# Lightning attention and an ELU layer on one core: attention in 64-token blocks on 64x64 tiles of TensorE

## The chip, the cores and the metric

The kernel runs on one core of a Trainium2 chip. The metric is the device time of one execution in microseconds (us); less is better. A core has TensorE (PE in the profile, its weight loads PEld), VectorE (DVE), ScalarE (ACT), GpSimd (POOL) and SyncE (SP, which here only starts transfers). Matmuls write PSUM, which has eight banks of 128 partitions x 512 float32.

## The reference

Four batches, eight heads, 768 tokens, 64 dimensions a head. Attention with a decay `lam` per head runs over blocks of 64 tokens and carries a 64x64 state per head; its output, 3072 tokens of 512, goes through two matrix products with an ELU between them.

```python
Dmask = np.where(rel >= 0, lam[:, None, None] ** rel[None, :, :], 0.0)
lam_pow = lam[:, None, None] ** (pos[None, :, None] + 1)
for b in range(nb):                       # nb = 768 // 64
    intra = np.einsum('bhic,bhjc->bhij', qb, kb) * Dmask[None]
    intra = np.einsum('bhij,bhjd->bhid', intra, vb)
    inter = np.einsum('bhid,bhde->bhie', qb * lam_pow[None], kv_state)
    out[:, :, sl] = intra + inter
    kb_dec = kb * rev_pow[None]           # lam ** (63 - pos)
    kv_state = lam_block * kv_state + np.einsum('bhsd,bhse->bhde', kb_dec, vb)
x = attn_out.transpose(0, 2, 1, 3).reshape(3072, 512)
h = x @ w_in                              # 512 x 2048
g = np.where(h > 0.0, h, np.exp(np.minimum(h, 0.0)) - 1.0)
out = g @ w_out                           # 2048 x 512
```

The block length of the decay is free: with the mask and the decays made for it, blocks of 128 tokens give the same result as blocks of 64.

## The kernel before

The tokens are cut into 24 chunks of 128. Chunk `g` is place `g // 4` in the sequence of batch `g % 4`, so chunks 0 to 3 are the first of each batch and have no state to read. The program is one long string of words, `PROGRAM`, written out in the order in which instructions are handed to the engines; every engine takes its own in that order, and waits at each until its operands and its buffer are there. A letter names the step and the number the chunk; what stands after `@` is the PSUM bank.

For one chunk:

- `Lq`, `Lk`, `Lv` load queries, keys and values with a cast to float16, started on POOL's queue (L240), for one chunk or for two at a time. `H` and `C` load one raw on SP and cast it on an engine. `wi`, `wo` load the weights in eight pieces each (L245, L251).
- `T` transposes q and k on PE (L264), and `tq`, `tk` take them out of PSUM (L272, L276). From chunk 8 on, transposing transfers on SP's queue do this (`Dq`, `Dk`, L280).
- `S`: scores, per head a 64x128 by 128 matmul (L287). Two heads lie one above the other in the 128 partitions, so a pair uses the upper and the lower half of the array's rows, and writes two banks. `s`: the decay mask, on DVE (L294).
- `P`: masked scores by values (L304), and the state by q (L310). Both give 64 columns of output a head, and a pair of heads uses the left and the right half of the array's columns. `p`: the result times `qs` into `xt`, on DVE (L328), or a copy on ACT where `tq` has scaled q already (L326).
- `kd`: keys times their decay, on POOL (L332). `U`: the update of the state, keys by values (L366, 64 columns; L354 on the whole array). `M`: the state times its decay, on POOL (L342). `u`: their sum, on DVE (L381).

Then for a group of chunks (`GROUPS`: the first four alone, the others two by two): `A`, the first product (L392), eight matmuls of 256 columns into one bank for a group of two; `x`, exp on ACT (L400); `r`, relu in place on ACT (L403); `m`, the ELU from both, on DVE (L408), into one of 40 `g` buffers. `B`, the second product (L422), four matmuls of 512 columns of one chunk. `o` takes the result out of PSUM (L431), `st` stores it from SP's queue. The last chunk is cut in 384 and 128 columns, the latter being `R` (L445).

`A` alternates between two banks of its own (tag `H`), `B` between `M0` and `M1`, and attention uses `A` to `D`. The loads wait for their buffers on POOL's queue in the order of the string, between `kd` and `M`; the transposing transfers and the stores do so on SP's.

Of the kernel before, what the change touches and what calls it, by code (L numbers as in the profile page):

```python
# [7 lines left out]
FP32 = mybir.dt.float32  # L8
FP16 = mybir.dt.float16
# [5 lines left out]
GROUPS = [(0, 1), (1, 1), (2, 1), (3, 1), (4, 2), (6, 2), (8, 2), (10, 2), (12, 2), (14, 2), (16, 2), (18, 2), (20, 2), (22, 2)]  # L15

LOADS = [(0, 1), (1, 1), (2, 1), (3, 1), (4, 2), (6, 2), (8, 2), (10, 2), (12, 2), (14, 2), (16, 2), (18, 2), (20, 2), (22, 2)]

BUFS = {'qn1': 4, 'kn1': 4, 'vn1': 4, 'qn2': 4, 'kn2': 4, 'vn2': 4, 'qT': 5, 'kT': 5, 'pp': 6, 'kd': 8, 'stt': 8, 'xt1': 4, 'xt2': 2, 'xt4': 2, 'e': 3, 'g': 40, 'osb512': 4}

ON = {'z0.0', 'z2.0', 'z1.0', 'o23', 'z3.0'}
# [67 lines left out]
def kernel(  # L89
# [14 lines left out]
    L = 128  # L104
    NHP = H // 2
# [4 lines left out]
    FB = 4  # L110
# [4 lines left out]
    load_of = {g + i: (g, i) for g, n in LOADS for i in range(n)}  # L115
    load_n = dict(LOADS)
    words = PROGRAM.split()
    scaled = {int(w[2:]) for w in words if w[:2] == "tq"}
# [12 lines left out]
    st = [[const(f"st{b}_{i}", [128, NHP, 128], FP16) for i in range(2)] for b in range(B)]  # L131
# [4 lines left out]
    pos = const("pos", [128, 3])  # L136
    row = const("row", [128, 128])
    ident16 = const("ident16", [128, 128], FP16)
    causT = const("causT", [128, 128])
    dn = const("dn", [128, H])  # L140
    mask = const("mask", [128, H, 128])
    qs = const("qs", [128, NHP, 128])
    ks = const("ks", [128, H])
    upp = const("upp", [128, NHP])
# [8 lines left out]
    R = [slice(0, 64), slice(64, 128)]  # L153
    nat, raw, tr, psT, psS, pp, psO, xg = {}, {}, {}, {}, {}, {}, {}, {}
    kds, stt, psU, psH, es, gts, psM, osb = {}, {}, {}, {}, {}, {}, {}, {}
    done = set()
# [4 lines left out]
    def bank(tag, shape, dtype, name):  # L161
        return ps.tile(shape, dtype, tag=f"ps{tag}", name=name, bufs=2 if tag == "H" else 1)
# [8 lines left out]
    def make_qs(_):  # L171
        for hp in range(NHP):
            nc.scalar.activation(
                qs[:, hp, :], row[:], AF.Exp, scale=loglam_p[:, hp : hp + 1]
            )
# [5 lines left out]
    simple = {  # L181
        "lam": lambda _: nc.sync.dma_start(
            out=lam_b[:], in_=lam.unsqueeze(0).broadcast_to([128, H])
        ),
        "tab": lambda _: nc.scalar.preload_act_table_set("natural_log_exp_and_others"),
# [35 lines left out]
    def of(w, g):  # L221
        g0, i = load_of[g]
        return nat[w, g0][:, i]
# [303 lines left out]
```

## Time and profile before

| | |
|---|---|
| median of 3 runs | 214.75 us (214.7 to 216.03) |
| profiled execution, time | 215.01 us |
| profiled execution, span | 213.2 us |
| granted TensorE clock | 1.0 |
| PE busy | 199.2 us, 2048 matmuls |
| DVE busy | 129.6 us, 223 instructions |
| ACT busy | 127.9 us, 245 instructions |
| POOL busy | 96.6 us, 115 instructions |
| HBM read, written | 27.27 MB, 6.29 MB |

The span runs from the first to the last instruction of the profiled execution; its time is 1.8 us more. A row of a group has the line of the kernel, the engine, the operation, output and inputs by name with their shapes, and the count; then the busy time in us, the mean duration in ns, and how long the engine was idle just before these instructions, with what ended most of that. A row of the timeline has start and length in us, engine and line, and `xN` where N of a kind were merged. A row by stretches has the busy time of PE, PEld, DVE, ACT and POOL in it (each with its count), then the clock, the DMA share and GB/s. Ends of matmuls are modelled; their starts are recorded.

### The profile page before, as it was taken

The page shows a single profiled execution, that of the slowest core. Times are in us where ns is not written, and L with a number is a line of the kernel's source. Part 1 is how long each engine was busy: PE and PEld are TensorE (multiplying, and loading weights), DVE is VectorE, ACT ScalarE, POOL GpSimd, SP SyncE. Part 2 cuts the span into 40 slices and gives each one's busy share as a digit, 9 for nine tenths or more (in the row PEclk, how much of TensorE's full clock was granted, in tenths as well). Part 3 has the DMA queues.
Part 4 walks back from the last instruction along what each step waited for, and adds up shares of the span by engine and source line. Part 5 has one row for each costly group of instructions (what it writes and reads, how often), then busy time and mean ns, then how long its engine had stood idle before and what let it go on. Part 6 is the DMA issues. An engine that isn't in the chain of part 4 may idle for free.

```text
span 213.2 us, 5052 instructions
## 1 busy us (share of the span) xinstructions
PE 199.2 (93%) x2048; PEld 138.5 (65%) x2048; DVE 129.6 (61%) x223; ACT 127.9 (60%) x245; POOL 96.6 (45%) x115
## 2 busy tenths in 40 slices
PE   0599989999999999999989999999999999999994
PEld 0378767677677766767657677667666776666662
DVE  3877764385877866788538676366558665353321
ACT  4436766568776765585554865665674565556731
POOL 7999965599994995376902691000000000000000
PEclk9999999999999999999999999999999999999999
DMA  5999999999999999969997999146110000021042
GB/s 95 152 181 184 197 194 182 158 145 151 161 120 166 127 169 150 148 101 113 187 148 80 158 187 127 25 130 145 25 52 0 0 16 36 3 103 46 0 152 98
DMA packets 101976, 24.59 MB, mean 115 GB/s; under 512 B 92608, under 2 KB 99008, under 8 KB 101952
## 3 DMA queue, kind: packets, MB, share of 16 engines
q0 software_dynamic: 79760, 13.50, 83.5%
q1 hardware_dynamic: 22192, 10.76, 23.9%
q8 instruction: 16, 0.26, 0.5%
q14 instruction: 8, 0.07, 0.1%
HBM read 27.27 MB, written 6.29 MB: 157 GB/s over the span
## 4 chain that ended last, share of the span: by engine, by line
PE 64%; POOL 17%; DMA 15%; issue 1%; ACT 0%; SPq 0%; POOLq 0%
PE psM L422 29%; PE psH L392 28%; DMA kn<-in_k_dram 5%; DMA vn<-in_v_dram 4%; DMA qT<-qn 4%; POOL wi L245 3%; POOL kn L240 3%; POOL wo L251 3%; POOL kd L332 3%; DMA out_dram<-osb 3%; POOL qn L240 3%; PE psO L304 2%; POOL vn L240 2%; PE psO L310 2%; PE psS L287 2%
## 5 line engine op out<-in xcount | busy, mean ns | idle before, releaser
L408 DVE SCALAR_TENSOR_TENSOR g<-e,psH 128x512 f16<-128x512 f32 x96 | 65.6, 685 | 61.3 <-ACT psH L403 61.0
L392 PE MATMUL psH<-xt,wi 128*128 128x256 f16 (+1 forms) x896 | 97.6, 259 | 0.9 <-DMA wi<-in_moe_w_in_dram 0.8
L400 ACT ACTIVATE e<-psH 128x512 f32<-128x512 f32 x96 | 57.2, 596 | 67.4 <-PE psH L392 67.0
L422 PE MATMUL psM<-wo,g 128*128 128x512 f16 (+1 forms) x384 | 92.7, 377 | 0.2 <-ACT osb L431 0.2
L392 PEld LDWEIGHTS <-wi 128*128 128x128 f16 x896 | 77.5, 99 | 22.8 <-DMA wi<-in_moe_w_in_dram 1.3
L403 ACT ACTIVATE psH<-psH 128x512 f32<-128x512 f32 x96 | 56.9, 594 | 0.0
L422 PEld LDWEIGHTS <-g 128*128 128x128 f16 x384 | 36.4, 98 | 31.4 <-issue 0.4
L294 DVE TENSOR_TENSOR pp<-psS,mask 128x512 f16<-128x512 f32 x48 | 31.4, 682 | 7.6 <-PE psS L287 7.5
L332 POOL TENSOR_TENSOR kd<-kn,ks 128x512 f16<-128x512 f16 x20 | 20.8, 1049 | 13.0 <-DMA kn<-in_k_dram 12.5
L342 POOL TENSOR_TENSOR stt<-st,upp 64x256 f32<-64x256 f16 x32 | 19.6, 612 | 7.4 <-DVE st L381 5.9
L240 POOL DMA_DIRECT2D vn<-in_v_dram x14 | 15.7, 1121 | 9.0 <-PE psO L310 9.0
L431 ACT COPY osb<-psM 128x512 f32<-128x512 f32 x23 | 13.4, 588 | 5.7 <-PE psM L422 4.8
L240 POOL DMA_DIRECT2D kn<-in_k_dram x14 | 15.5, 1107 | 1.6 <-DMA wi<-in_moe_w_in_dram 1.4
L240 POOL DMA_DIRECT2D qn<-in_q_dram x13 | 14.4, 1110 | 0.1
L381 DVE TENSOR_TENSOR st<-stt,psU 64x256 f16<-64x256 f32 x32 | 13.0, 415 | 0.8 <-PE psU L366 0.3
L304 PE MATMUL psO<-pp,vn 128*64 128x128 f16 x192 | 12.5, 229 | 0.3 <-DMA vn<-in_v_dram 0.3
L304 PEld LDWEIGHTS <-vn 128*64 128x64 f16 x192 | 10.0, 114 | 2.6 <-issue 1.6
L328 DVE TENSOR_TENSOR xt<-psO,qs 128x512 f16<-128x512 f32 x16 | 10.7, 683 | 1.1 <-PE psH L392 0.6
L287 PE MATMUL psS<-qT,kT 64*128 64x128 f16 x192 | 8.4, 228 | 2.8 <-DMA qT<-qn 1.1
L310 PE MATMUL psO<-qT,st 128*64 128x128 f16 x160 | 10.3, 219 | 0.0
L287 PEld LDWEIGHTS <-kT 64*128 64x128 f16 x192 | 5.9, 98 | 5.8 <-issue 3.6
L310 PEld LDWEIGHTS <-st 128*64 128x64 f16 x160 | 9.0, 110 | 0.0
(45 smaller groups left out, 65.1 us busy)
## 6 DMA issues: line engine op xcount, KB each, us to landing
out_dram<-osb SPq DMA_DIRECT2D x23, 256.0 KB, 2.9
qn<-in_q_dram POOLq DMA_DIRECT2D x10, 256.0 KB, 8.0
kn<-in_k_dram POOLq DMA_DIRECT2D x10, 256.0 KB, 6.5
vn<-in_v_dram POOLq DMA_DIRECT2D x10, 256.0 KB, 7.0
wi<-in_moe_w_in_dram POOLq DMA_DIRECT2D x8, 256.0 KB, 6.4
wo<-in_moe_w_out_dram POOLq DMA_DIRECT2D x8, 256.0 KB, 7.4
kn<-in_k_dram POOLq DMA_DIRECT2D x4, 128.0 KB, 4.7
vn<-in_v_dram POOLq DMA_DIRECT2D x4, 128.0 KB, 5.5
```

The lines of the kernel that those rows point to most:

```text
L240: nc.gpsimd.dma_start(out=t[:].rearrange("p b h d -> p (b h) d"), in_=source(w, g0, load_n[g0]))
L287: nc.tensor.matmul(psS[g, hh][:, hp, :], lhsT=tr["k", g][r, hp, :], rhs=tr["q", g][r, hp, :], start=True, stop=True,)
L294: nc.vector.tensor_tensor(out=p[:], in0=psS.pop((g, hh))[:], in1=mask[:, hh::2, :], op=ALU.mult)
L304: nc.tensor.matmul(po[r, hp, :], lhsT=of("v", g)[:, 2 * hp + hh, :], rhs=pp[g, hh][:, hp, :], start=True, stop=(cb == 0), skip_group_check ...
L310: nc.tensor.matmul(po[r, hp, :], lhsT=st[b][cb % 2][:, hp, r], rhs=tr["q", g][:, hp, :], start=False, stop=True, skip_group_check=True,)
L332: nc.gpsimd.tensor_tensor(out=kds[g][:], in0=of("k", g), in1=ks[:].unsqueeze(2).broadcast_to([128, H, 64]), op=ALU.mult,)
L342: nc.gpsimd.tensor_tensor(out=t[r], in0=st[b][cb % 2][r, :, r], in1=upp[r].unsqueeze(2).broadcast_to([64, NHP, 64]), op=ALU.mult,)
L392: nc.tensor.matmul(pH[:, f * n * 128 : (f + 1) * n * 128], lhsT=wi16[i][:, kk, w * 128 : (w + 1) * 128], rhs=xg[g0][:, kk, :], start=(kk = ...
L400: nc.scalar.activation(es[g0, j][:], psH[g0, j][:], AF.Exp)
L403: nc.scalar.activation(psH[g0, j][:], psH[g0, j][:], AF.Relu)
L408: nc.vector.scalar_tensor_tensor(out=g[:].rearrange("p f c t -> p (f c t)"), in0=es.pop((g0, j))[:], scalar=-1.0, in1=psH.pop((g0, j))[:], ...
L422: nc.tensor.matmul(psM[g][:, cols], lhsT=gts[g, f], rhs=wo16[i][:, w, cols], start=f == 0, stop=f == NFT - 1, skip_group_check=True,)
```

## The change

Attention goes over to blocks of 64 tokens. Two chunks (two batches at the same place) are handled together, and in each the two halves of 64 tokens:

- A transpose takes the same head of both chunks, so the two batches lie one above the other in the 128 partitions (`transpose`, and `transpose_dma` in two halves). q, k are loaded chunk by chunk into interleaved tiles, v by two.
- Scores, masked scores by values, state by q and updates are matmuls of 64 rows, 64 columns of weights and 64 columns of data. Four in a row use the four quarters of the array. A chunk's mask is one operation of 512 in place of two.
- The state exists for each block of 64: `u` and `M` come twice per pair of chunks, each over all 128 partitions.
- In the first chunks no state is read: the second half of the tokens sees the first through a score block of its own (`mask1` for the whole 128 keys, `z` for the first half).
- `Q` is the state by q for one assignment of halves, ahead of `P`; `F`, a copy of one column on DVE, stands between them.
- All groups are of two chunks. 31 of the 96 relus go to DVE, 7 of the `o`, 6 of the 12 `kd`. All PSUM tiles share eight banks that the string names one by one.
- `W`: 36 products with zeros on PE in the opening.
- The whole order is new.

```diff
-GROUPS = [(0, 1), (1, 1), (2, 1), (3, 1), (4, 2), (6, 2), (8, 2), (10, 2), (12, 2), (14, 2), (16, 2), (18, 2), (20, 2), (22, 2)]
+GROUPS = [(0, 2), (2, 2), (4, 2), (6, 2), (8, 2), (10, 2), (12, 2), (14, 2), (16, 2), (18, 2), (20, 2), (22, 2)]
...
+BUFS = {'qn': 5, 'kn': 5, 'vn': 6, 'qT': 3, 'kT': 3, 'pp': 6, 'kd': 3, 'state': 6, 'stt': 3, 'xt2': 3, 'xt4': 2, 'e': 3, 'g': 40, 'osb512': 4}
...
+    "Lk0 Lk1 wz W0@0 W1 W2 W3 W4 W5 W6 W7 W8 W9 W10 W11 W12 W13 W14 W15 W16 Lv0 iota Lq2 tab Hq0 "
+    "Lq3 Lk2 Lk3 wi2 lam wi7 Cq0 pos1 row Lv2 wi0 wi1 wi6 wi5 Lk4 pos0 idn pos5 cau1 Lk5 wi3 pos2 "
+    "pos3 ln dn1 dn wo0 Lq4 Tka0@1 cau pos4 ks kd2 msk1 llp msk Lq5 wi4 Hq1 Cq1 tka0 Tqa0@2 tqa0 "
+    "Tqb0 tqb0 Tkb0 tkb0 wo6 qs W17 W18 W19 W20 kd0 S0@3,4,5,6 s0 W21 W22 W23 Tq2@7 W24 s1 z1 z0 "
+    "W25 W26 W27 W28 W29 tq2 Tk2@1 P0@2,3 p0.0 W30 W31 tk2 W32 W33 W34 S2@4,6,7,5 p0.1 W35 A0:7@1 "
...
+        r = slice(half * NHP, (half + 1) * NHP)
+        rows = slice(half * H, (half + 1) * H)
+        nc.sync.dma_start_transpose(
+            out=tr[w, g][:, r, :], in_=full[w, g][:, rows].rearrange("p a d -> p (a d)")
+        )
...
     def scores(g, banks):
+        for i in range(2):
+            psS[g + i] = bank(banks[i], [128, H, LB], FP32, f"psS{g + i}")
+        if g < B:
+            for i in range(2):
+                psZ[g + i] = bank(banks[2 + i], [128, H, LB], FP32, f"psZ{g + i}")
+            for h in range(H):
+                for kb, qb in ((1, 1), (0, 1), (0, 0)):
+                    for i, d in enumerate(R):
+                        nc.tensor.matmul(
+                            (psS if qb else psZ)[g + i][R[kb], h, :],
+                            lhsT=tr["k", g][d, h, R[kb]], rhs=tr["q", g][d, h, R[qb]],
+                            start=True, stop=True, skip_group_check=True,
+                        )
+            return
+        for h in range(H):
+            for i, d in enumerate(R):
+                for s in R:
+                    nc.tensor.matmul(
+                        psS[g + i][s, h, :], lhsT=tr["k", g][d, h, s], rhs=tr["q", g][d, h, s],
+                        start=True, stop=True, skip_group_check=True,
+                    )
...
     def products(g, banks):
...
+        for i in reversed(range(2)):
+            for hp in range(NHP):
+                for s, rs in enumerate(R):
+                    for c, rc in enumerate(R):
+                        nc.tensor.matmul(
+                            psO[g, s][rc, i, hp, :], lhsT=vof(g + i)[rs, 2 * hp + c, :],
+                            rhs=pp[g + i][rs, 2 * hp + c, :], start=False, stop=False,
+                            skip_group_check=True,
+                        )
+        state_products(g, 0)
+
+    def state_products(g, part, banks=None):
...
+        for hp in reversed(range(NHP)):
+            for i, d in enumerate(R):
+                s = i ^ part
+                for c in reversed(range(2)):
                     nc.tensor.matmul(
+                        psO[g, s][R[c], i, hp, :],
+                        lhsT=state[b, 2 * cb + s][d, 2 * hp + c, :],
+                        rhs=tr["q", g][d, 2 * hp + c, R[s]],
+                        start=(part == 1 and hp == NHP - 1), stop=part == 0, skip_group_check=True,
                     )
 
+    def fence(g):
+        t = buf("fence", [128, 1], FP32, f"fence{g}")
+        nc.vector.tensor_copy(t[:], psO[g, 0][:, 1, 0, :1])
...
+    def update_products(g, banks):
+        for x, bk in enumerate(banks):
+            psU[g, x] = bank(bk, [128, H, 64], FP32, f"psU{g}_{x}")
+        for h in range(H):
+            for s in range(len(banks)):
+                for i, d in enumerate(R):
                     nc.tensor.matmul(
+                        psU[g, s][d, h, :], lhsT=kds[g][R[s], h, i, :], rhs=vof(g + i)[R[s], h, :],
                         start=True, stop=True, skip_group_check=True,
                     )
...
+    def zeros_product(k, banks):
+        if k == 0:
+            idle.append(bank(banks[0], [128, 512], FP32, "psW"))
+        nc.tensor.matmul(
+            idle[1][:, : WARM[k]], lhsT=idle[0][:, :128], rhs=idle[0][:, : WARM[k]],
+            start=True, stop=True,
+        )
```

After the change PE has 36 products with zeros, 48 transposes, 96 scores, 64 products of pp and v in the first chunks, then 320 scores, 320 products of pp and v, 320 of state and q, 352 updates, 768 first products of 256 columns, 384 second products and the 16 of `R`.

More of the change, by code (lines that the diff above doesn't have):

```diff
@@ L104 @@
     L = 128
+    LB = 64
     NHP = H // 2
@@ L153 @@
     R = [slice(0, 64), slice(64, 128)]
+    HALF = {"": slice(None), "a": slice(0, 2), "b": slice(2, 4)}
+    HEADS = {"": range(H), "a": range(H // 2), "b": range(H // 2, H)}
     nat, raw, tr, psT, psS, pp, psO, xg = {}, {}, {}, {}, {}, {}, {}, {}
     kds, stt, psU, psH, es, gts, psM, osb = {}, {}, {}, {}, {}, {}, {}, {}
+    state, full, early, psZ, ppz = {}, {}, {}, {}, {}
     done = set()
@@ L196 @@
         "cau": lambda _: nc.vector.tensor_scalar(
[L197 removed]
+            out=causT[:], in0=row[:, :LB], scalar1=pos[:, 2:3], scalar2=None, op0=ALU.is_ge
         ),
@@ L282, in scores, with transpose @@
-    def scores(g, banks):
-        for hh in range(2):
-            psS[g, hh] = bank(banks[hh], [128, NHP, 128], FP32, f"psS{g}_{hh}")
-        for hp in range(NHP):
-            for hh, r in enumerate(R):
-                nc.tensor.matmul(
-                    psS[g, hh][:, hp, :], lhsT=tr["k", g][r, hp, :], rhs=tr["q", g][r, hp, :],
-                    start=True, stop=True,
-                )
-    def masked(g, hh):
-        p = pp[g, hh] = buf("pp", [128, NHP, 128], FP16, f"pp{g}_{hh}")
-        nc.vector.tensor_tensor(
-            out=p[:], in0=psS.pop((g, hh))[:], in1=mask[:, hh::2, :], op=ALU.mult
-        )
+    def transpose(w, part, g, banks):
+        if banks[0]:
+            psT[w, g] = bank(banks[0], [128, H, 128], FP16, f"psT{w}{g}")
+        for h in HEADS[part]:
+            nc.tensor.transpose(
+                psT[w, g][:, h, :], in_=of(w, g)[:, h, :, :], identity=ident16[:]
+            )
@@ new lines, in evacuate_t, with transpose_dma @@
+    def evacuate_t(w, part, g):
+        if (w, g) not in tr:
+            tr[w, g] = buf(f"{w}T", [128, H, 128], FP16, f"{w}T{g}")
+        r = HEADS[part]
+        dst = tr[w, g][:, r.start : r.stop, :]
+        src = psT[w, g][:, r.start : r.stop, :]
+        if f"t{w}{part}{g}" in ON:
+            nc.vector.tensor_copy(dst, src)
+        else:
+            nc.scalar.copy(out=dst, in_=src)
+    def transpose_dma(w, g, half):
+        if (w, g) not in tr:
+            tr[w, g] = buf(f"{w}T", [128, H, 128], FP16, f"{w}T{g}")
+        r = slice(half * NHP, (half + 1) * NHP)
[3 more added lines that the diff above has]
+        )
@@ new lines, in masked, with masked_first, out_banks @@
+    def masked(g):
+        p = pp[g] = buf("pp", [128, H, LB], FP16, f"pp{g}")
+        m = mask1 if g < B else mask
+        nc.vector.tensor_tensor(out=p[:], in0=psS.pop(g)[:], in1=m[:], op=ALU.mult)
+    def masked_first(g):
+        p = ppz[g] = buf("pp", [128, H, LB], FP16, f"ppz{g}")
+        nc.vector.tensor_tensor(out=p[R[0]], in0=psZ.pop(g)[R[0]], in1=mask[R[0]], op=ALU.mult)
+    def out_banks(g, banks):
+        for s in range(2):
+            psO[g, s] = bank(banks[s], [128, 2, NHP, LB], FP32, f"psO{g}_{s}")
@@ L369, in update_products, with decay_state @@
                         start=True, stop=True, skip_group_check=True,
                     )
-    def update(g, hh):
+    def decay_state(g, s):
         cb, b = divmod(g, B)
-        r = R[hh]
-        assert cb > 1 or f"z{b}.{(cb + 1) % 2}" in done
-        assert cb == 0 or (f"P{g - B}" in done and f"M{g}" in done)
-        new = st[b][(cb + 1) % 2][r, :, r]
-        if cb == 0:
-            nc.vector.tensor_copy(new, psU.pop((g, hh)))
+        t = stt[g, s] = buf("stt", [128, H, 64], FP32, f"stt{g}_{s}")
+        nc.gpsimd.tensor_tensor(
+            out=t[:], in0=state[b, 2 * cb + s][:],
+            in1=upp[:].unsqueeze(2).broadcast_to([128, H, 64]), op=ALU.mult,
+        )
@@ L380, in update, with first_product @@
+    def update(g, s):
+        cb, b = divmod(g, B)
+        n = 2 * cb + s
+        new = state[b, n + 1] = buf("state", [128, H, 64], FP16, f"state{b}_{n + 1}")
+        if n == 0:
+            nc.vector.tensor_copy(new[:], psU.pop((g, s))[:])
         else:
             nc.vector.tensor_tensor(
-                out=new, in0=stt.pop((g, hh))[r], in1=psU.pop((g, hh)), op=ALU.add
+                out=new[:], in0=stt.pop((g, s))[:], in1=psU.pop((g, s))[:], op=ALU.add
             )
-    def first_product(g0, j):
+    def first_product(g0, j, banks, part=slice(None)):
@@ L386, in first_product @@
         n = size_of[g0]
-        assert {f"p{g0 + i}" for i in range(n)} <= done
-        pH = psH[g0, j] = bank("H", [128, FB * 128], FP32, f"psH{g0}_{j}")
-        for f in range(FB // n):
+        assert {f"p{g0 + i}.{x}" for i in range(0, n, 2) for x in range(2)} <= done
+        if banks[0]:
+            psH[g0, j] = bank(banks[0], [128, FB * 128], FP32, f"psH{g0}_{j}")
+        pH = psH[g0, j]
+        for f in range(FB // n)[part]:
             i, w = divmod(j * (FB // n) + f, 2)
@@ L414, in elu, with second_product @@
                 gts[g0 + c, j * (FB // n) + f] = g[:, f, c, :]
-    def second_product(g, j, banks):
+    def second_product(g, j, banks, part=slice(None)):
         cols = slice(0, CUT if g == LAST else DM)
-        if j == 0:
+        if banks[0]:
             psM[g] = bank(banks[0], [128, DM], FP32, f"psM{g}")
-        for f in range(j * FB, (j + 1) * FB):
+        for f in range(j * FB, (j + 1) * FB)[part]:
             i, w = divmod(f, 2)
```

266 lines of the change are left out of this document (133 added, 133 removed), and 104 rows, old and new, of the table PROGRAM.

## The prediction

> **What bounds the kernel now.** I read the page from the top: busy shares, then the groups of instructions, then the timeline of three short stretches, then busy time by stretches of 20 us.
>
> ```profile
> PE 199.2 (93%) x2048; PEld 138.5 (65%) x2048; DVE 129.6 (61%) x223; ACT 127.9 (60%) x245; POOL 96.6 (45%) x115
> ...
> PE   0599989999999999999989999999999999999994
> ...
> L408 DVE SCALAR_TENSOR_TENSOR g<-e,psH 128x512 f16<-128x512 f32 x96 | 65.6, 685 | 61.3 <-ACT psH L403 61.0
> ...
> L403 ACT ACTIVATE psH<-psH 128x512 f32<-128x512 f32 x96 | 56.9, 594 | 0.0
> L294 DVE TENSOR_TENSOR pp<-psS,mask 128x512 f16<-128x512 f32 x48 | 31.4, 682 | 7.6 <-PE psS L287 7.5
> L332 POOL TENSOR_TENSOR kd<-kn,ks 128x512 f16<-128x512 f16 x20 | 20.8, 1049 | 13.0 <-DMA kn<-in_k_dram 12.5
> L342 POOL TENSOR_TENSOR stt<-st,upp 64x256 f32<-64x256 f16 x32 | 19.6, 612 | 7.4 <-DVE st L381 5.9
> ```
>
> PE is busy from the second slice to the last; DVE and ACT sit idle some 40% of the time, nearly all of it waiting for PE or for each other. So PE's own work counts, and what keeps PE waiting at both ends. A group's busy time holds the depth of the pipe at each burst's end, so I price matmuls by the step from one start to the next, from merged rows of the timeline (start, length, engine, line, count):
>
> ```profile
> 14.39 2.85 PE L392 MATMUL psH<-xt,wi 128*128 128x128 f16 x32
> ...
> 19.13 1.95 PE L392 MATMUL psH<-xt,wi 128*128 128x128 f16 x32
> ...
> 143.01 0.27 PE L392 MATMUL psH<-xt,wi 128*128 128x256 f16 x1
> 143.21 0.69 PE L366 MATMUL psU<-vn,kd 128*64 128x64 f16 x32
> 143.74 0.23 PE L304 MATMUL psO<-pp,vn 128*64 128x128 f16 x2
> 143.80 0.22 PE L310 MATMUL psO<-qT,st 128*64 128x128 f16 x2
> 143.85 0.22 PE L304 MATMUL psO<-pp,vn 128*64 128x128 f16 x2
> ```
>
> To be seen: the two half-width matmuls of a pair (x2) start together, and the next pair 0.056 us later, the step that a single 128-wide matmul has. 32 matmuls of 64 columns take 0.69 less one length (0.197), over 31 steps: 15.9 ns each, 31.5 ns a pair. From the last whole-array matmul (143.01) to the first on half tiles (143.21) are 0.20 us where 0.109 is its own step, so a change of tile shape costs 0.09 to 0.095. The chain of waits has 16 psH matmuls in 1.75 (0.109 each) and 8 psM in 1.73 (0.216).
>
> **PE before.** First and second product: 640 x 0.109 + 256 x 0.057 + 368 x 0.216 + 16 x 0.163 + 0.9 = 167.5. Attention: 96 pairs of scores, 96 of pp by v, 80 of state by q, each 0.056: 15.2; 64 update pairs at 0.0315 and 16 whole ones: 2.9; 64 transposes at 0.056: 3.6; 53 changes of tile shape: 5.0. Sum 194.2. The span is 213.2; the other 19 us are 6.1 before the first matmul, 3.0 after the last, and waits and a slow opening. The execution took 215.01, which is 1.8 over its span and 0.12% over the median of 214.75.
>
> **PE after.** Groups are all of two chunks: 768 x 0.109 + 368 x 0.216 + 16 x 0.163 + 0.9 = 166.7, or 0.8 less. Attention has 1,472 matmuls on 64x64 tiles, 64 columns each: 320 + 96 scores, 320 + 64 pp by v, 320 state, 352 updates. Outside the first chunks they stand in the order as 328 sets of four, one for each quarter of the array, rows of different halves writing different PSUM banks. The trace has no set of four. It has column pairs (L304, L366) and row pairs (L287), and in both the second matmul starts 3 to 4 ns after the first and costs nothing. One end: a set of four steps as the 64-column pair does, 31.5 ns. Other end: two pairs in turn, 63 ns. Below the first end there is little: 64 columns are half the 0.056 step, 28 ns, 1.1 us in all. I take 31.5, since each half of a set is a row of this trace: 328 x 0.0315 = 10.3. The first chunks' scores use one quarter twice per head (32 steps) and their products are 32 pairs: 2.0. 48 transposes: 2.7. 42 changes of shape: 4.0. Sum 166.7 + 10.3 + 2.0 + 2.7 + 4.0 = 185.7, which is 8.5 under before.
>
> **The other engines.** DVE loses 24 of the 48 masks and gains 31 relus (nearest row the elu, 0.685; bounds 0.56, the 384-wide copy, and 0.69), 7 evacuations of psM, 6 decays of keys (128x1024; 1.23 by the mask's row of that shape, bounds 0.7 and 1.4), 24 xt in place of 16, and 22 whole state updates (0.42 to 0.69; I take 0.68 as for the masks) in place of 40 halves: 65.8 + 21 + 16.4 + 2.7 + 16.4 + 15 + 7.4 + 4.7 + 1.5 (ten fences, 0.15 each) + 6.5 of set-up and copies = 157, up 28. ACT falls to 116. POOL: 46 single loads at 0.9, 12 double at 1.17, 16 weights at 0.77 make 68; 6 decays at 2.1, 13; 20 state decays 128x512 (0.61 to 1.22; the kd row of that size says 1.05), 22. Sum about 102, up 6. None of the three sets the end as long as its results are ready when PE asks: that cover is the order's. Per 10 us of PE work along the new order DVE has 14, 11, 8, 9, 9, 9, 11, 9, 9, 9, 8, then under 9.5: nearly full for the first 115 us of PE work, where before, after a first 14, has 3 to 12.
>
> SP has 36 transposing transfers in place of 32 and the same stores; loads bring the same 64-element rows. The fence between state products and pp products makes PE's later instructions wait for DVE: 0.2 of drain, 0.15, and up to 0.69 of DVE's queue. Mostly updates, scores or first products stand between; where none does (three places) I count 0.5 each, and all that is queued behind on PE waits too.
>
> **The opening.** In before the first psH starts at 14.39. In after k0 and k1 are issued first (1.25 and 2.15; a single key load lands 4.7 after issue: 6.9), and q0, q1 come by SP (3.5: about 5). But iota is now behind three loads on POOL, at 4.6 where it ended at 2.56, and DVE's list is long: constants and two masks to 8.5, copies of kT to 9.75, kd0 to 11.0, four masked scores to 13.7, the products, two xt to 16.0. So the first psH at 16.0, 1.6 later, for two chunks at once. The 36 products with zeros (30 x 0.216 + 6 x 0.109 = 7.1, more while the clock is low) lie in PE's idle time ahead of that; each costs at most its 0.2 if an operand is early. They should spare the slow steps of the opening (2.85 against 1.95 for the same 32 matmuls).
>
> **Sum.** Before: 14.4 to the first psH; by then PE has done 5.2 of 194.2, so 189.0 remain, and 3.0 of tail: 206.4. The span is 213.2, so waits after the first psH are 6.8. After: 16.0; 4.1 done, 181.6 remain; tail 3.0: 200.6. The waits I take as before, 6.8: the second pair's masks hold PE about a microsecond at 18, the fences 1.5, and the rest is evacuation while the weights come in. Span 207.4, with 1.8 around it 209.2.
>
> **The rivals.** A measurement tells about 1% from no change, so faster is under 212.6 and slower over 216.9.
>
> (a) DVE becomes the bound, slower than before. By the order's place where PE has done 114 us, DVE must have done 104; PE would be there at about 126, DVE begins at 6, so DVE has to hold 87%. That is the point from which it decides. The stretches speak for it:
>
> ```profile
> 60.00:80.00 20.00, 20.00 (x206) 13.88 (x205) 15.33 (x29) 13.18 (x25) 16.85 (x20) 1.00 1.77 144
> 80.00:100.00 20.00, 19.81 (x232) 14.05 (x230) 15.01 (x26) 12.12 (x23) 10.95 (x13) 1.00 1.24 126
> ```
>
> The third busy figure is DVE's: 77% at most in 20 us, though nothing asked for more there. At 82% it arrives at 6 + 104/0.82 = 133: 7 late, time 217. Against it: forty g buffers let PE choose second products that are ready.
>
> (b) Sets of four run as two pairs: 328 x 0.0315 more, 10.3: 219.5. The change then does not do what its tiles promise. The overlap of pairs in both directions speaks against it.
>
> (c) PE's front end cannot hand out a matmul and its weight load every 8 ns. The densest stretch here is the 64 matmuls from 143.21 to 144.58, 21.7 ns each, and only the first 32 were at 15.9; the new order has runs of 112 and 192. At 21.7 the 1,472 take 32.0 instead of 12.3: 229. For it: nothing faster was sustained. Against: that stretch shows no stall, its pace is that of its columns.
>
> [...]
>
> (d) The order keeps PE fed: waits of 2 after the first psH: 204.4.
>
> **How the numbers follow.** Forecast (waits between 3 and 10, so 205 to 212.5) 0.58; (d) 0.10; (a) 0.15; (b) 0.10; (c) 0.07. The likeliest time is 209. Faster: 0.53 of the forecast, 0.10 of (d), 0.02 of (a): 0.65. Same: 0.05 and 0.05 of (a): 0.10. Slower: 0.08 of (a), 0.10, 0.07: 0.25. The range from 203 to 220 holds (d) to (b) and leaves out (c) and ends of the others.
>
> **What would show it.** Right: 31 to 33 ns from one set of four to the next on the lines of scores, products and updates; first psH near 16; DVE near 157, ACT near 116; after the first psH some 7 us of PE idle. Wrong: 60 ns a set (b); weight loads and matmuls evenly spaced through the long runs with idle put down to issue (c); PE idle put down to DVE's g, pp or xt (a); PE waiting for qT, kT or vn, since loads and transposes in single chunks come later than I take.

## The result, and the profile after

The kernel after takes 213.15 us (median of 20 runs, 212.03 to 216.83) against 214.5 for the kernel before (20 runs, 213.1 to 216.03). The ratio is 0.9938, 95% interval 0.9912 to 0.9964: faster by 0.6%, which by the bound named in the prediction is no change. 209.0 was forecast; the direction was right, and less than a quarter of the gain came.

The profiled execution took 216.83 with a span of 214.9 and is one of the longest of the 20. No shorter execution of this kernel was profiled. The runs cold and late_loads below, profiled at 213.28 and 214.58, have its order from the first psH to 140 us: there the stop near 62 us, 3.8 here, lasts 3.2 and 3.0, and that near 90 us, 2.75 here, only 0.6 and 0.8.

The lines of the page that answer to those shown of before (busy time and share; busy tenths of 40 slices; the clock granted to PE; the queue that fetches instructions; then groups with busy time and mean ns, and idle time before them):

```profile
PE 201.7 (94%) x2724; PEld 135.6 (63%) x2724; DVE 144.9 (67%) x242; ACT 103.4 (48%) x196; POOL 99.1 (46%) x106
...
PE   7798999999948999879999999999999999999993
...
PEclk9999999999995999999999999999999999999999
...
q8 instruction: 21, 0.34, 0.7%
...
L520 PE MATMUL psM<-wo,g 128*128 128x512 f16 (+1 forms) x384 | 90.7, 380 | 3.7 <-issue 3.7
...
L506 DVE SCALAR_TENSOR_TENSOR g<-e,psH 128x512 f16<-128x512 f32 x96 | 62.7, 682 | 19.5 <-ACT psH L501 18.8
...
L412 PE MATMUL psO<-qT,state 64*64 64x64 f16 x320 | 6.1, 196 | 2.6 <-issue 2.6
```

PE is again busy from end to end, but the twelfth slice of its row (59.1 to 64.5 us) has a 4, and the clock in the next slice a 5. DVE does 144.9, less than the 157 forecast, and two PE groups have idle time that ended by "issue", that is, by nothing that the profile shows. The waits of PE after the opening, in the same execution (total, times, longest):

```profile
PE psM L520 <- issue: 3.7, 1, 3.7
PE psO L412 <- issue: 2.6, 1, 2.6
...
PE psO L383 <- issue: 0.6, 1, 0.6
PE psO L383 <- DVE ppz L362: 0.3, 1, 0.3
```

So nearly all waiting is three single stops, each put down to no engine. The timeline around the first (start, length, what):

```profile
60.74 0.43 PE L454 MATMUL psU<-vn,kd 64*64 64x64 f16 x32
61.27 0.45 PE L395 MATMUL psO<-pp,vn 64*64 64x64 f16 x32
61.52 0.32 PE L412 MATMUL psO<-qT,state 64*64 64x64 f16 x16
65.54 1.01 PE L520 MATMUL psM<-wo,g 128*128 128x512 f16 x2 [3.70 <-issue]
```

and busy time by stretches (PE, PEld, DVE, ACT, POOL, then the clock, the DMA share, GB/s):

```profile
57.00:61.70 4.70, 4.61 (x174) 2.64 (x162) 4.56 (x9) 0.00 (x0) 2.62 (x3) 1.00 1.90 185
61.70:65.50 3.80, 0.14 (x19) 0.12 (x5) 1.58 (x3) 0.00 (x0) 2.93 (x3) 0.81 1.80 88
65.50:71.00 5.50, 5.46 (x23) 3.21 (x23) 1.19 (x2) 0.74 (x2) 0.87 (x1) 0.51 2.12 180
```

Two things are to be seen. A block of 32 matmuls on quarters lasts 0.45, less one length (0.20) over 31 steps: 8.1 ns each, 32 a set of four, as forecast. And after a dense stretch of them PE stands for 3.7 us, and nothing that the profile shows holds it: the weights of its next matmul are loaded at 61.77, ACT does nothing in that time, and DVE's last operation ends at 63.3, 2.2 before PE goes on. Then the clock is at half for 6.8 us, from 64.1 to 70.9; PE works from 65.54 on, so this costs it half of 5.4, some 2.7 more.

What the three stops share is a number. I count PE's matmuls and weight loads together, in the order of their starts, and with them the 21 semaphore waits and drains that PE's sequencer has among them. The stops lie after 449, 1729 and 2497 of them, each 193 above a multiple of 256, and nowhere else. The instruction queue moved 21 packets of 16 KB for 5469 such instructions (16 for 4110 in the kernel before, whose row is below): that is one for 260 and one for 257, so about one packet for 256, which I call a page.

```profile
q8 instruction: 16, 0.26, 0.5%
```

For each boundary the trace gives when the page ahead of it began to run, when the packet for the next page moved, and when PE went on:

| kernel, boundary | page runs from | used up | lasts | POOL's loads open then | packet moves | starts after page's start | PE goes on | stop |
|---|---|---|---|---|---|---|---|---|
| after, 449 | 12.51 | 19.09 | 6.58 | 8 | 17.48 to 18.41 | 4.97 | 19.89 | 0.80 |
| after, 1473 | 45.01 | 57.20 | 12.19 | 6 | 46.82 to 47.71 | 1.81 | 57.20 | 0 |
| after, 1729 | 57.20 | 61.77 | 4.57 | 8 | 62.31 to 63.71 | 5.12 | 65.54 | 3.77 |
| after, 2497 | 84.79 | 90.15 | 5.36 | 6 | 89.81 to 91.44 | 5.02 | 92.90 | 2.75 |
| after, 4545 | 150.14 | 155.76 | 5.62 | 0 | 151.00 to 152.38 | 0.86 | 155.76 | 0 |
| before, 1473 | 58.87 | 70.46 | 11.59 | 1 | 59.69 to 60.88 | 0.82 | 70.47 | 0 |

(Open is a load that POOL has issued and that has not landed when the page begins to run.) Where PE stopped, it went on 1.5 to 1.8 us after the packet had landed. A page that is used up before that makes PE stand. In the kernel before no page lasts under 9.37 us, and PE stops at no boundary (the longest step across one is 0.21); with small matmuls at 8 ns a page shrinks to 4.6.

My theory is then: PE stops where a page of 256 instructions is used up before the next has come, and the fetch comes late because it queues behind the loads. The rival: the work at those places waits for something else, for banks, for operands or for the change of shape. A second rival is that the sets of four are at fault as such.

### The profile page after: what moved, and what is told of

The parts are those of the page before. It is cut to its first block, busy times and chain, and to the rows that moved or that the text cites. A ratio compares the mean times of both kernels' runs of the same rounds, so it can differ in the third digit from the quotient of the medians.

```text
span 214.9 us, 6336 instructions
## 1 busy us (share of the span) xinstructions
PE 201.7 (94%) x2724; PEld 135.6 (63%) x2724; DVE 144.9 (67%) x242; ACT 103.4 (48%) x196; POOL 99.1 (46%) x106
## 4 chain that ended last, share of the span: by engine, by line
PE 85%; issue 5%; DVE 4%; DMA 3%; ACT 1%; POOL 0%; DVEq 0%; ACTq 0%; POOLq 0%
PE psH L487 39%; PE psM L520 36%; DMA kn<-in_k_dram 3%; PE psW L547 2%; PE psO L412 2%; PE psO L395 2%; PE psU L454 2%; PE psS L350 1%; DVE g L506 1%; DVE psH L499 1%; DVE pp L358 1%; PE psO L383 1%; PE psTq L308 1%; PE psTk L308 1%; DVE ppz L362 1%
## 5 line engine op out<-in xcount | busy, mean ns | idle before, releaser
L487 PE MATMUL psH<-xt,wi 128*128 128x256 f16 x768 | 92.6, 276 | 0.0
L462 POOL TENSOR_TENSOR stt<-state,upp 128x512 f32<-128x512 f16 x20 | 21.5, 1080 | 39.1 <-DVE state L474 36.2
L501 ACT ACTIVATE psH<-psH 128x512 f32<-128x512 f32 x65 | 37.8, 595 | 0.0
L499 DVE TENSOR_SCALAR psH<-psH 128x512 f32<-128x512 f32 x31 | 21.3, 694 | 18.3 <-ACT e L495 18.2
L529 ACT COPY osb<-psM 128x512 f32<-128x512 f32 (+1 forms) x17 | 9.9, 580 | 31.1 <-PE psM L520 31.1
L358 DVE TENSOR_TENSOR pp<-psS,mask 128x512 f16<-128x512 f32 x24 | 15.5, 682 | 1.9 <-PE psS L350 1.4
L474 DVE TENSOR_TENSOR state<-stt,psU 128x512 f16<-128x512 f32 x20 | 13.4, 679 | 1.3 <-PE psU L454 1.2
L442 POOL TENSOR_TENSOR kd<-kn,ks 128x1024 f16<-128x1024 f16 (+1 forms) x6 | 11.4, 1905 | 2.4 <-DMA kn<-in_k_dram 2.4
L547 PE MATMUL psW<-zeros 128*128 128x512 f16 (+1 forms) x36 | 10.5, 442 | 1.2 <-DVE zeros L540 1.2
L412 PE MATMUL psO<-qT,state 64*64 64x64 f16 x320 | 6.1, 196 | 2.6 <-issue 2.6
L442 DVE TENSOR_TENSOR kd<-kn,ks 128x1024 f16<-128x1024 f16 x6 | 7.8, 1294 | 0.0
L412 PEld LDWEIGHTS <-state 64*64 64x64 f16 x320 | 4.3, 107 | 5.2 <-issue 4.4
```

The lines of the kernel that those rows point to most:

```text
L358: nc.vector.tensor_tensor(out=p[:], in0=psS.pop(g)[:], in1=m[:], op=ALU.mult)
L442: (nc.vector if f"kd{g}" in ON else nc.gpsimd).tensor_tensor(out=kds[g][r], in0=of("k", g)[r], in1=ks[r].unsqueeze(2).unsqueeze(3).broadca ...
L462: nc.gpsimd.tensor_tensor(out=t[:], in0=state[b, 2 * cb + s][:], in1=upp[:].unsqueeze(2).broadcast_to([128, H, 64]), op=ALU.mult,)
L487: nc.tensor.matmul(pH[:, f * n * 128 : (f + 1) * n * 128], lhsT=wi16[i][:, kk, w * 128 : (w + 1) * 128], rhs=xg[g0][:, kk].rearrange("p a ...
L499: nc.vector.tensor_scalar_max(psH[g0, j][:], psH[g0, j][:], 0.0)
L501: nc.scalar.activation(psH[g0, j][:], psH[g0, j][:], AF.Relu)
```

## Experiments

Ratios are against the kernel before, run on the same chip.

**again**: the kernel after, unchanged, to see whether the stops return.

> The changed kernel as it is, for a profile of an execution without a second half-clock stretch and for a time on the same chip as the next three. Both theories: 213, the stalls again before the last matmuls of B5:3 and inside P10, 1 to 4 us each, since how long a fetch takes varies from execution to execution.

212.92 us, ratio 0.992 (0.9874 to 0.9965). The waits, in an execution of 216.57:

```profile
PE psM L520 <- issue: 3.1, 1, 3.1
PE psO L412 <- issue: 2.4, 1, 2.4
```

The same places, again at 1729 and 2497, with half clock from 63.9 to 70.7. The places are a property of the program, not of one execution; the length of the second stop is not, as cold and late_loads show.

**shift120**: the same work with 120 more PE instructions before the first real one.

```diff
+        cuts = 4 if 5 <= k < 25 else 1
+        for c in range(cuts):
+            cols = slice(c * WARM[k] // cuts, (c + 1) * WARM[k] // cuts)
             nc.tensor.matmul(
-                idle[1][:, : WARM[k]], lhsT=idle[0][:, :128], rhs=idle[0][:, : WARM[k]],
+                idle[1][:, cols], lhsT=idle[0][:, :128], rhs=idle[0][:, cols],
...
```

> Twenty of the 512-wide products with zeros in the opening are cut into four of 128: the same PE time, 60 matmuls and so 120 PE instructions more, nothing else touched. Theory F (instruction pages): PE's instructions are fetched in pages of 256 over the same DMA engines as the loads, the next page takes 5 to 9 us to come while the loads run, and PE stands still when it uses up a page sooner. Then the two stalls of the changed kernel (3.9 us at 61.7, before the last matmuls of B5:3, and 2.7 us at 90.1, inside P10) leave their words and new ones appear at other words, 120 instructions earlier in the order counted from a page's start (pages under 6 us then end in P4, U8, P8 and at A10:0), 2 to 5 us each; time above the changed kernel by 2 to 9 us: 215 to 222. Theory W (a wait for an operand or a bank that the trace does not name): the stalls stay at B5:3 and inside P10, time 213.

221.13 us, ratio 1.0302 (1.0212 to 1.0391).

```profile
PE psO L412 <- issue: 3.0, 1, 3.0
PE psU L454 <- issue: 2.9, 1, 2.9
PE psO L395 <- issue: 2.4, 1, 2.4
...
PE psO L412 <- DMA qT<-qn: 1.1, 1, 1.1
```

The old places are free of stops. New ones stand inside blocks of like matmuls, where the trace names no wait (L412 to L412, U to U, L395 to L395), at 2241, 3521 and 4801, again 193 above multiples of 256, after pages of 4.54, 3.02 and 1.34 us. The same arithmetic in the same order takes 8 us more than the kernel after. Of the profiled executions (221.24 and 216.83) it has 9.9 us of stops at boundaries for 7.3, a wait of 1.1 for a transfer, and a first psH 0.4 later. The rival of banks and operands falls. The last of the three also shows that a prompt fetch doesn't save a page that is short enough: it began 0.73 after the page's start, and PE still stood 2.59.

**spread**: other work is put between the dense stretches; nothing is added.

```diff
- U8@5,2 F6 st2 P6 B5:3 Dq8.1 Lk16 A4:4@1 Dk10.0 ... r6:0 r4:4 ... r6:3 B4:3 m6:3
+ B4:3 U8@5,2 F6 st2 A4:4@1 P6 B5:3 Dq8.1 Lk16 Dk10.0 ... r6:0 r4:4 ... r6:3 m6:3
- U12@6,5 Lq17 Dk16.0 P10 p10.0 ... A8:4@1 Lk20 A8:1@3 x8:1
+ A8:4@1 U12@6,5 Lq17 Dk16.0 A8:1@3 P10 p10.0 ... Lk20 x8:1
```

> Four words of PE's order are moved up into the two dense stretches where it stood still: B4:3 before U8, A4:4 before P6, A8:4 before U12, A8:1 before P10. Same instructions, same work. Theory F: each dense page lasts 1.7 us longer on useful work, so the stall of 3.9 us falls to about 2.2 and that of 2.7 to about 1; the first then is under the length that let the clock drop to half for 6.8 us, so the granted clock is 0.998. Time 208.5 to 211. Theory W: the waits stay at their words, 213 or more, since products that were ready are only done earlier.

212.36 us, ratio 0.9889 (0.9846 to 0.9932), where 208.5 to 211 was expected. The stop at 1729 is down to 1.51, that at 2497 gone, one at 2241 has 0.47, and the clock stays at 1.0; but the order now has three waits of its own (0.5 for `g`, 0.4 and 0.8 for `xt`).

**spread2**: as spread, with `A8:1` left where it was, behind P10.

> As the run with four words moved up, but A8:1 stays behind P10, so that PE has work while DVE takes P10's result out (PE waited 0.8 us for xt there). Theory F: the page at B5:3 stalls about 1.5 us, the one in P10 about 1, no wait for xt: 0.5 us under that run, 1.5 to 2.5 under the changed kernel on this chip. Theory W: as the changed kernel.

212.4 us, ratio 0.989 (0.9845 to 0.9934). The waits of PE after the first 20 us:

```profile
PE psO L412 <- issue: 1.1, 1, 1.1
...
PE psH L487 <- DVE g L506: 0.5, 1, 0.5
PE psH L487 <- DVE xt L430: 0.4, 1, 0.4
PE psU L454 <- DMA vn<-in_v_dram: 0.4, 1, 0.4
```

The page ahead of 1729 now lasts 6.25 in place of 4.57, 1.7 longer, and the stop is 1.27, 2.5 shorter (the fetch also began 0.2 earlier, took 0.4 less, and PE went on 0.2 sooner after it). What the moves free they partly give back as ordinary waits. Beside again, on the same chip, the medians differ by 0.5 us only, within both intervals, where 1.5 to 2.5 was expected.

**pairs**: the loops of scores, `pp` by `v` and updates take all heads of one half before the other, so that no four quarters follow each other.

```diff
-        for h in range(H):
-            for i, d in enumerate(R):
-                for s in R:
+        for s in R:
+            for h in range(H):
+                for i, d in enumerate(R):
...
```

> The loops of scores, pp products and updates outside the first chunks go over the halves outside: a whole half's pairs, then the other half's. The same 992 matmuls, but two quarters of the array at work at a time in place of four. If the quarters are worth what the trace says (32 ns for a set of four), 248 sets take 63 ns: 7.8 us more PE work, of which the two dense pages that stalled give back some 0.7 each: time 218 to 221 and about 4 ns, 28 ns as the alternating steps. If PE's supply of instructions sets the pace of attention in general, the time stays at 213.

215.53 us, ratio 1.0025 (0.9991 to 1.0059). The dense place again:

```profile
61.41 0.32 PE L412 MATMUL psO<-qT,state 64*64 64x64 f16 x16
61.56 0.58 PE L454 MATMUL psU<-vn,kd 64*64 64x64 f16 x32
```

32 updates last 0.58 in place of 0.43 to 0.46: 12.3 ns each and not 8.1, neither overlap of four nor of two (15.9). Some 31 such blocks cost an estimated 4.7 us more PE work, of which about 2.4 shows against the kernel after (218 to 221 was expected). The stops are shorter here (2.80 at 1729, none at 2497, where the fetch began 3.0 after its page's start in place of 5.0), but how much of the difference that makes is not separated. The stop at 1729 stands without any set of four, so the second rival, that the sets are at fault as such, falls. So the order by quarters earns what its tiles promise, and rival (b) of the prediction is what happens without it, at less than its price.

**cold**: the 36 products with zeros in the opening are 64 columns wide.

```diff
-WARM = [512, 512, ... 512, 256, 256, 256, 256, 256, 256]
+WARM = [64] * 36
```

> The 36 products with zeros get 64 columns each in place of 512 and 256: the same instructions and pages, but nearly no PE time. If they are worth what the prediction says (the slow steps of the opening), the first transposes step at 0.107, the clock comes up only after the first psH, the first psH is about 0.5 us later and 1 to 2 us are lost in all: 214.5 to 216. The page that ends in P2 is 2.5 us shorter, so the stall there (0.8 us) may grow by up to that much as well. If the zeros were only filler, 212.5 to 213.5.

212.56 us, ratio 0.9896 (0.9855 to 0.9937); my expectation of a loss was wrong. PE now waits 5.9 us for the first keys, as the profile shows,

```profile
PE psTk L308 <- DMA kn<-in_k_dram: 5.9, 1, 5.9
PE psM L520 <- issue: 3.1, 1, 3.1
```

and the first psH starts at 16.79 in place of 16.6. The slow steps of the opening that the zeros were to spare are in the traces: the first products of the kernel before step by 0.107 us until 16.29 and by 0.056 from 16.36 on, the zeros of 512 columns in the kernel after by 0.427 until 5.86 and by 0.216 from 6.18 on; the profile gives the granted clock there as 1.0 throughout. But as long work the zeros were worth nothing here. The stops are 0.64, 3.21 at 1729 and 0.56 at 2497, with one stretch of half clock of 3.41 us.

**minus24**: twelve of the zero products are left out, which moves every boundary 24 instructions later in the work.

```diff
+        if 5 <= k < 17:
+            return
```

> Twelve of the 36 products of zeros in the opening (numbers 5 to 16) are left out, and nothing else: PE hands out 24 instructions fewer before the first real one, so every boundary between its pages of 256 moves 24 instructions later in the work. The order stays as it is. By the trace of the kernel after, the shortest page before 110 us would then last 5.4 us (near 74 and 80 us) instead of 4.6 (at 57 us). Page theory: the stall at 61.7 us (3.2 to 3.8 us) is gone or under 0.8; one at the boundaries near 80 us may appear, 0 to 2 us, depending on how long after its page's start the fetch begins (2.9 to 5 us there); the sum of stalls falls from about 6 us to 0.5 to 3, and the time to 209 to 211.5, ratio 0.973 to 0.984. Rival (the work at U8 and P6 waits by itself, for banks or operands): the stalls stay at the same work, and the time stays at 212.5 to 213.5, ratio 0.992 to 0.996. The missing zeros alone should cost nothing: the kernel with narrow zeros (cold) was as fast.

213.38 us, ratio 0.9881 (0.9811 to 0.9951). The boundaries moved as reckoned: the short page at 57 now lasts 6.12 and its stop is 1.54 (forecast under 0.8), and the page before 80.4, 5.38 long, has a new one of 1.29. There the fetch was later than in the kernel after (4.3 after its page's start, for 2.9). And 2497, after a page of 5.39, keeps 2.18. The sum of stops fell from 7.3 to 5.0, where 0.5 to 3 was expected, and the time is the same as after's, not the 209 to 211.5 expected: in the profiled execution the first keys came later and the first psH at 17.9. The place of each boundary was right, the length of the stops was not: it hangs on when the fetch begins, which varies.

**spread2_8**: the order of spread2 and eight more instructions in the opening (four zero products cut in two, as in shift120).

> The order of spread2, and four of the zero products cut in two, so that PE hands out 8 instructions more before the first real one: the boundaries lie 8 instructions earlier in the work. The shortest page before 110 us would last 5.9 us (near 73 us) instead of 5.4, and the one at 56 us 6.2 as in spread2. Page theory: stall near 63 us 1 to 1.6 us as in spread2, all others under 0.3: 211.5 to 212.5, ratio 0.985 to 0.990, the same as spread2 within 0.5%. Rival (each shift of the boundaries gives a new, unrelated time): a difference of more than 1% to spread2.

212.11 us, ratio 0.9857 (0.9796 to 0.9919), the lowest median of all and within 0.5% of spread2. It beats the kernel before; against the kernel after the intervals overlap. The stops are 1.52 at 1729, 0.88 at 2497, and 1.29 at 449 in the opening; the last two were expected under 0.3.

**late_loads**: what makes the fetch late? In the kernel after it begins at most 1.6 us after the page's start from 101 us on, where at most three of POOL's loads stand open, and pages of 5.6 and 6.1 us there don't stop PE. Twelve extra loads of `v`, which nothing reads, go behind POOL's last work on a state, into a tile with two buffers.

```diff
- M22.0 x12:6
+ M22.0 X0 X1 X2 X3 X4 X5 X6 X7 X8 X9 X10 X11 x12:6
+    def extra(_):
+        t = sb.tile([128, 16, 64], FP16, tag="scr", name="scr", bufs=2)
+        nc.gpsimd.dma_start(out=t[:], in_=source("v", 20, 2))
...
```

> Twelve loads of two value chunks each, into a tile that nobody reads, are added on POOL's queue after its last state decay but one (at about 147 us), when the DMA engines of the changed kernel are nearly quiet. PE's pages from 150 to 162 us are as dense (5.6 and 6.1 us for 256 instructions) as those that stalled at 62 and 90, but did not stall. Theory F: with the DMA engines loaded their fetches take 5 us and more in place of 1 to 2, and PE stands still for 1 to 3 us near 156 and near 162, put down to issue; time up by 1 to 6 us. Theory W: nothing waits for these loads, no new stall, time as the changed kernel's.

214.11 us, ratio 0.9964 (0.991 to 1.0017). The DMA engines are 90% busy or more in most of the stretch from 148 to 160 us, the fetches begin 2.24 and 1.01 after their pages' starts, and no new stop appears. A busy DMA alone doesn't delay the fetch by 5 us. But with two buffers at most two extra loads stand open (2, 1 and 2 when the three pages from 148 us on begin), which I had overlooked.

**late_loads2**: 24 extra loads, ten of them ahead of M22.0.

> The late loads once more, this time ten before POOL's last state decay (from about 133 us) and fourteen behind it, so that several loads are outstanding when PE enters the pages at 148 and 153 us. In the first form the DMA engines were busy there but little was outstanding, and the fetches began 1 to 2.2 us after PE entered a page. If what delays a fetch is the backlog of transfers already handed to the DMA engines, they now begin 4 to 5 us after, as they do near 57 and 65 us, and PE stands still 1 to 3 us at one or both of the page ends near 153 and 159. If it is something else in the earlier part, they begin after 1 to 2.2 us as before and there is no stall.

228.64 us, ratio 1.0635 (1.0554 to 1.0717), and no answer. The ten loads held POOL back from the state:

```profile
PE psO L412 <- DVE state L474: 11.1, 1, 11.1
```

and still only two stood open at a time. The fetches began 1 to 2 us after their pages' starts.

**late_loads3**: the twelve loads of late_loads, each into a tile of its own, so that POOL issues them without waiting.

```diff
-        t = sb.tile([128, 16, 64], FP16, tag="scr", name="scr", bufs=2)
-        nc.gpsimd.dma_start(out=t[:], in_=source("v", 20, 2))
+        scr.append(sb.tile([128, 16, 64], FP16, tag=f"scr{len(scr)}", name=f"scr{len(scr)}", bufs=1))
+        nc.gpsimd.dma_start(out=scr[-1][:], in_=source("v", 20, 2))
```

> The order of the kernel after with twelve extra loads of v (256 KB each, the same shape as its own) behind POOL's last update of a state, each into a tile of its own, so that POOL issues them one after the other from about 146 us without waiting for the one before: four to eight stand issued and not landed while the dense pages of 5.6 and 6.1 us (from 150 to 162 us) run. Nothing reads them. In the kernel after these pages don't stall: the fetch of the next begins about 1 us after the page is entered, where before 95 us it begins 2.5 to 5 us after. Theory 1 (the fetch of PE's instructions waits behind the loads that stand issued): the fetches near 153 and 159 us begin 3 to 5 us after their page is entered, with stalls of 0.5 to 3 us at one or both, and the time rises by 1 to 4 us. Theory 2 (what delays the early fetches is something else, such as the place in the program): they begin within 2.3 us as in the two runs with loads one at a time, and no stall over 0.3 us appears; the time stays within 1 us of the kernel after's.

214.8 us, ratio 1.0005 (0.9964 to 1.0046), 1.65 above the kernel after. From 144.0 POOL issues nine loads, one each 1.15 us, then three more, and when the pages from 147.2, 152.9 and 160.7 us begin, 2, 6 and 5 of them stand open. The lines of the trace for the extra loads (from issue to landing), for PE's waits from 140 us on (the kernel after has none there), and for the timeline near 159:

```profile
DMA to landing us min/median/max: 4.9/10.8/12.5
```

```profile
PE psH L487 <- issue: 1.6, 1, 1.6
```

```profile
157.79 1.36 PE L487 MATMUL psH<-xt,wi 128*128 128x256 f16 x11
160.71 0.72 PE L487 MATMUL psH<-xt,wi 128*128 128x256 f16 x5 [1.56 <-issue]
```

The fetches of these pages' successors now begin 2.99, 5.32 and 4.06 after their pages' starts (0.86, 1.62 and -0.74 in the kernel after, with no load open), and at 4801, after a page of 6.02 us, PE stands 1.83 us amid sixteen psH matmuls of one kind. Of the other kernels only shift120 stopped PE at a boundary in that stretch, after a page of 1.34 us. PE's program and boundaries are those of the kernel after, and the twelve loads are those of late_loads, which handed them over two at a time and had fetches at 2.24 and 1.01: it is the loads that stand open that delay the fetch here. This settles the theory's second half, in one profiled execution: the lags grow with the open loads (2.24 and 1.01 to 5.32 and 4.06). By what mechanism no run shows.

## Why the prediction was wrong

By its own steps, in the profiled execution and, for the waits, in the median run (213.15, so a span of about 211.1):

| term | forecast | measured |
|---|---|---|
| first psH | 16.0 | 16.6 |
| PE work left after it | 181.6 | 182.8 |
| waits after it, profiled execution | 6.8 | 12.1 |
| waits after it, median run | 6.8 | 8.3 |
| after the last matmul | 3.0 | 3.4 |
| around the span | 1.8 | 2.0 |

PE's work is again a sum of steps: the forecast's 181.6 and the 1.2 by which attention's steps came out longer. The waits are what is left of the span when the other terms are taken off (214.9 - 16.6 - 182.8 - 3.4 = 12.1).

**Right: PE's work.** Sets of four step by 32 ns (31.5 forecast). Attention took 16.2 where 15.0 was reckoned, by the same method of steps. Rival (b) doesn't occur: 8.1 ns a matmul were measured over whole blocks of 32. The opening came 0.6 late, close to its estimate.

**Right in outcome, but too high: the other engines.** DVE has 144.9 for 157, ACT 103.4 for 116, POOL 99.1 for 102. Rival (a) needed DVE at 87%; it never became the bound, and no wait of PE for it after the opening is over 0.3 us.

**The step that failed: "The waits I take as before, 6.8".** The prediction filled them with the second pair's masks (1 us), three fences of 0.5 and evacuation. Those came to at most 2.1 in all: of the 12.1 in the profiled execution 7.3 are the three stops at page boundaries and 2.7 the half clock after the first, and of the 2.1 that remain the trace names 0.3 as a wait. late_loads3 splits the same way: stops of 2.90, 0.47, 0.79 and 1.83, half clock 2.8, and a rest of 2.0 make its 10.8; and so does cold, whose span of 211.2 is near the median run's: stops of 4.4, half clock 1.7 and a rest of 2.1 make its 8.2. So a number carried over from the kernel before came out near enough in sum, 8.3 in the median run, by luck, and was wrong in every part. The prediction gave some 7 us of idle PE as a sign of being right; the profiled execution has them too, but they are the stops.

In the kernel before, too, the 6.8 was what a sum left over and not waits that the trace names. After the first psH these come to 2.4, of which the largest are

```profile
PE psS L287 <- DMA qT<-qn: 1.1, 1, 1.1
PE psH L392 <- DMA wi<-in_moe_w_in_dram: 0.8, 1, 0.8
```

and 0.9 more is the first 32 psH, at 2.85 for 1.95. Of evacuation the trace names 0.2 only; the rest stays open.

Without the stops and the half clock the time would have been 16.6 + 182.8 + 2.1 + 3.4 + 2.0 = 206.9: rival (d), an order that keeps PE fed, was right about the order (its waits of 2 against the rest of 2.1), and the fetch took it back. That figure is worked out; no run reached it.

**Rival (c) had the right place and the wrong price.** It asked whether PE's front end can hand out a matmul and a weight load every 8 ns, and priced a slow pace for each matmul. The pace is kept for blocks of 32 and more; what fails is the supply, once for a page of 256, in this kernel only where the page is short and loads stand open (in shift120 also after a page of 1.34 us with none). The trace of before had the row that bears on it: 16 packets on the instruction queue, each begun at most 2.8 us after the start of a page that lasts 9.37 or more. I read none of it, since a queue with 0.5% of the DMA time looked like nothing.

Of the miss of 4.0 us (213.15 for 209.2), 1.5 are the waits' sum, 1.2 PE's work, 0.6 the opening, 0.6 the tail and what is around the span. spread and spread2 show that another order can shrink the stops, and that it gives part of this back as waits of its own. That a stop costs about its length is shown where stops were added (shift120, late_loads3); where they shrank (spread, spread2, minus24) the time fell by less or not at all, and no run shows the whole gain. Two small sums of the prediction are off, with no effect on the verdict: the products of before add up to 167.3, not 167.5, and (a), 7 late, would be 216, not 217.

## What to carry to other kernels

When a change makes instructions shorter, count them: a page of 256 PE instructions (128 matmuls with their weight loads) has to last as long as its successor's fetch, here 3.9 us with no load open (shift120: a page of 1.34 and a stop of 2.59) and up to 8.3 us behind a backlog of six to eight loads (the kernel after, from 57.20 to 65.54). The change did both: the page that begins near 57 us lasts 4.6 in place of 11.6, with eight loads open in place of one. An idle PE put down to "issue" with nothing late is a sign of it; the index of the instruction modulo 256, counted with those of PE's sequencer, tells it from a wait. And a term taken over from the kernel before should be split into its causes first, for the change may remove all of them and add another.

## What the runs showed of the hardware

- In the profiles of before, after, late_loads and late_loads3 the fetch of PE's next 256 instructions begins at most 2.3 us after the current page's start where none or one of POOL's loads is open, and 1.8 to 5.3 after it where six or more are. It takes 0.9 to 1.8, and over all runs a stopped PE goes on 1.4 to 1.9 after it. It is a tendency: minus24 and shift120 each have one that began 1.0 to 1.2 after its page's start with six open, and spread2 one that began 3.2 after it with one open.
- Cutting work into 120 more PE instructions cost 8 us (shift120, 221.13 for 213.15), leaving out 24 nothing (minus24, 213.38), adding 8 to another order nothing (spread2_8, 212.11 for spread2's 212.4): the time of this kernel can depend on its count of instructions.
- Four quarters of the array in turn step at 8.1 ns (the kernel after, from 61.27), the same kind of matmuls half by half at 12.3 (pairs, from 61.56).
- In these runs, after stops of 2.8 to 3.8 us the clock is at half for one or two stretches of 3.41 us, and a whole one through which PE works costs it 1.7; after spread2's 1.27 it isn't. The length alone doesn't decide: after 2.18 in minus24 there was one such stretch, after 2.6 to 2.75 in again, shift120 and the kernel after none. So a stop of 2.18 us is not safe here; what decides no run shows.
- What stays open is which packets a fetch waits behind, and so why it began 2.9 us after a page's start in one execution and 4.3 in another at nearly the same place.
